# The first load of queries and keys in one transfer or in five, before an attention and two MoE layers on one core

## The chip, the core and the metric

One core of a Trainium2 chip runs one program. The metric is the device time of one execution in microseconds (us), as a median over runs. Beside the timed runs there is one execution taken with the hardware profiler; all rows below come from that one.

## The reference, cut to what matters

Inputs are float32. Attention has 2 batches of 12 heads, 448 positions and head size 64, with a causal mask. Its output, 896 tokens of 768 features, goes through two feed-forward layers that are plain matrix products.

```python
scores = (1 / sqrt(64)) * q @ k.T;  scores[above the diagonal] = -1e9
attn = exp(scores - max);  attn = attn / (sum(attn) + 1e-9)
x = attn @ v                                    # (896, 768) over all heads
h = x @ w_in;  g = max(h, 0) + alpha * min(h, 0);  x = g @ w_out      # 768 -> 2048 -> 768
h = max(x @ w1, x @ w2, x @ w3);  out = h @ w_out2                    # 768 -> 768 -> 768
```

## The kernel before, in words

The kernel takes the attention in 12 jobs, one for each pair of heads (class `Job`, line 560). A pair sits on the two halves of the 128 partitions: head 0 on rows 0 to 63 and head 1 on rows 64 to 127, 64 being the head size. The queries of a head are cut into four chunks, chunk 0 of 64 rows and chunks 1 to 3 of 128. Chunk `c` needs only the first 192, 320 or 448 keys (c = 1, 2, 3), since the mask hides the rest. For head 1 the keys are stored in reverse order.

A job loads one tile `qk` of 128 x 960 values (480 KB, line 681) and one tile `v` (line 685), both from the SyncE queue. Its scores (line 701) are products of 64 rows, both heads side by side, in groups of chunks. The first job takes its groups in the order 1, 2, 3, 0; the others take (3), (2, 1), 0. Chunk 0 of both heads is one pair of products over all 128 rows (`first_scores`, line 717). VectorE then takes the row maxima under the mask (line 735), ScalarE the exponentials (line 748), VectorE the reciprocals of the sums (lines 761 and 762), GpSimd scales the rows (line 766), TensorE transposes them (line 791), and the product with `v` follows (line 812). Scores go into four PSUM banks (`RINGS["s"]`), two for each group, so the third group waits until the maxima of the first have been read. The `qk` tile has three buffers.

After the attention come the feed-forward products (line 503), in two float32r parts for each operand. While the attention runs, the conversion of the first weights (lines 463 to 498) fills ScalarE, VectorE and GpSimd.

At the very start TensorE runs nine products of constants, 448 bfloat16 columns each (`warm`, line 877, `WARM = 9`). Nobody reads their result. Meanwhile GpSimd makes the identity and the masks (lines 277 to 305), and ScalarE loads its table for the exponential.

The order of instructions on every engine is fixed when the program is built, by a list planner (class `Plan`, line 76). Each step has a rank, a set of engines with its cost on each, the steps that it comes after, and the ring buffers that it takes and gives back. The planner keeps a clock for each engine and picks over and over the step that can start first, and of those that start within 0.02 us of each other the one of lowest rank. A step's `delay` is added after its cost before others may follow it. `NONE` is an engine without instructions. The chip does not know these times; it runs each engine's list in order and waits on semaphores. For a load of `qk` the planner reckons 0.05 + 480/285 = 1.73 us of SyncE and a delay of 1.8 us.

Two jobs are started ahead of the one whose probabilities are transposed (`LEAD = 2`). SyncE's list begins with `qk` of job 0, `qk` of job 1, `v` of job 0, `qk` of job 2 and `v` of job 1.

Of the kernel before, what the change touches and what calls it, by code (L numbers as in the profile page):

```python
# [11 lines left out]
F32 = mybir.dt.float32  # L12
# [11 lines left out]
RINGS = dict(w=4, s=4, t=3, a=1, v=4, qk=3, e=3, p=2)  # L24
LEAD = 2
NB = 3
HELD = 3
WARM = 9


RANK = dict(
    load=-6, v=12, s=12, max=12, exp=16, recip=10,
# [15 lines left out]
def f32(ap):  # L48
    return ap.bitcast(F32)


def step(fn, *args):
    return lambda engine: fn(*args)
# [6 lines left out]
def on_act(n, psum=False, words=False):  # L60
    return {"ACT": (0.056 if psum else 0.1) + n * (0.92e-3 if words else 0.833e-3)}
# [10 lines left out]
def on_dma(kb):  # L72
    return {"SP": 0.05 + kb / 285}
# [129 lines left out]
def attention_moe_moe2_kernel(  # L203
# [24 lines left out]
    nc = tc.nc  # L228
    B, HP = qk.shape[:2]
    D = 64  # L230
    DM, NT = out.shape
    S = NT // B
    DFF = alpha.shape[0] * alpha.shape[1]
    DF2 = w1.shape[0] * w1.shape[3]
    P = 128
# [8 lines left out]
    START = [0, *range(S % P, S + 1, P)]  # L244
# [19 lines left out]
    first = attn.enter_context(tc.tile_pool(name="first", bufs=1))  # L264
    ld = attn.enter_context(tc.tile_pool(name="ld", bufs=3))
# [16 lines left out]
    for j in range(2):  # L282
        nc.gpsimd.affine_select(
            out=short[P // 2 * j : P // 2 * j + P // 2],
            in_=short[P // 2 * j : P // 2 * j + P // 2],
# [7 lines left out]
    for j, o in enumerate((S - P, 0)):  # L293
# [3 lines left out]
            out=mask[:, o : o + P],  # L297
            in_=mask[:, o : o + P],
# [12 lines left out]
        delay=1.8,  # L311
# [222 lines left out]


    H = P // 2
    assert ROWS[0] == H and ROWS[1:] == [P] * (NCH - 1) and NCH == 4
    PLACES = [
        [1, 0, (0, 2, 3), (0, 0, 1), (0, 0, 2), (0, 0, 3), (0, 1, 2), (0, 1, 3)],
# [12 lines left out]

    e_all = [at.tile([P, 2 * NP - H], F32, bufs=1, name=f"e{i}") for i in range(RINGS["e"])]
    used = {"e": 0}

    def turn(name, tiles):
        used[name] += 1
        return tiles[(used[name] - 1) % len(tiles)]

    class Job:  # L560


        def __init__(self, rank, b, hp, after):
            self.b, self.hp, self.rank = b, hp, rank
            self.ps, self.pt, self.p = {}, {}, {}

            self.groups = ((1,), (2,), (3,), (0,)) if rank == 0 else ((3,), (2, 1), (0,))
            sums = ((1,), (2,), (3, 0)) if rank == 0 else ((3,), (2, 1, 0))
            self.sums = {cs[-1]: cs for cs in sums}
            self.slot = {c: k for k, c in enumerate(c for cs in sums for c in cs)}  # L570

            add = self.add
            self.load = add("load", on_dma(480), step(self.load_qk), take=("qk",), delay=1.8)
            self.norm, self.exps, self.max, s = {}, {}, {}, None
            for i, cs in enumerate(self.groups[:-1]):
                s = add(
                    "s",
                    {"PE": 4 * sum(START[c + 1] for c in cs) / 2400},
                    step(self.scores, i),
                    (self.load, *after) if s is None else (s,),  # L580
                    take=("s", "s") + ("e",) * (i == 0),
                    mode="rows",
                )
                if i == 0:
                    self.e_took = s
                if 3 in cs:
                    self.shared = s
                self.soften(s, cs, s)

            self.scored = s  # L590

        def add(self, kind, *args, **kw):
            return plan.add(self.rank + RANK[kind], *args, **kw)
# [40 lines left out]
        def turn(self, after, spare):  # L634
# [3 lines left out]
            for i in range(2):  # L638
# [11 lines left out]
                for k in range(2):  # L650
                    w = BANK if i == 0 or k else 6 * H
                    self.outs.append(
# [10 lines left out]
        def sum(self, after):  # L663
            add = self.add
            load_v = add("v", on_dma(448), step(self.load_v), take=("v",), delay=1.8)
            self.summed = a = add(
                "av",
                {"PE": 4 * (sum(S - START[kc + 1] for kc in range(NCH - 1)) + NCH * H) / 2400},
                step(self.av),
                [*self.outs, load_v, *after],  # L670
                take=("a",),
                give=(("p", self.p_took), ("v", load_v)),
                mode="columns",
            )
            hi, lo = (partial(self.x_out, i) for i in range(2))
            src = lambda: self.pv
            x = add("x", on_act(S, psum=True), copy(hi, src), (a,))
            self.done = add("x", on_dve(S, psum=True), sub(lo, src, hi), (x,), give=(("a", a),))

        def load_qk(self):  # L680
            self.qk = ld.tile([P, 2 * S + P // 2], F32, tag="qk", bufs=RINGS["qk"], name="qk")
            nc.sync.dma_start(out=self.qk, in_=qk[self.b, self.hp])

        def load_v(self):
            self.v = ld.tile([P, 2 * NCH - 1, 2, D], F32, tag="v", bufs=RINGS["v"], name="v")
            nc.sync.dma_start(out=self.v, in_=v[self.b, self.hp])

        def scores(self, i):
            if i == 0:
                self.e = e_all[used["e"] % len(e_all)]  # L690
                self.nm = at.tile([P, NCH, 2], F32, tag="nm", bufs=RINGS["e"], name="nm")
                self.sm = turn("e", sm_all)
                self.rm = at.tile([P, NCH, 2], F32, tag="rm", bufs=RINGS["e"], name="rm")
            banks = [ps_s.tile([P, BANK], F32, tag="s", name="ps") for _ in range(2)]
            o = 0
            for c in self.groups[i]:
                n = START[c + 1]
                for j in range(2):
                    d = slice(D * j, D * j + D)
                    self.ps[c, j] = banks[j][:, o : o + n]  # L700
                    nc.tensor.matmul(  # L701
                        self.ps[c, j],
                        self.qk[d, H + START[c] : H + START[c] + P],
                        self.keys(n, j)[d],
                        start=True,
                        stop=True,
                    )
                o += n
            if 3 in self.groups[i]:
                self.ps[0, 0] = banks[0][:, S:]  # L710

        def keys(self, n, j):
            return self.qk[:, 2 * S + H - n :] if j else self.qk[:, S + H : S + H + n]

        def first_scores(self):
            for j in range(2):
                nc.tensor.matmul(
                    self.ps[0, 0][H * j : H * j + H],
                    self.qk[:, H * j : H * j + H],
                    self.keys(H, j),  # L720
                    start=True,
                    stop=True,
                )
# [150 lines left out]
    def warm():  # L874
        ps = ps_a.tile([P, BANK], F32, tag="a", name="warm")[:, :S]
        for _ in range(WARM):
            nc.tensor.matmul(ps, ones[:, :P], ones, start=True, stop=True)  # L877

    plan.add(0, {"PE": WARM * 0.36}, step(warm), take=("a",), give=(("a", None),))
    places = [(b, hp) for b in range(B) for hp in range(HP)]  # L880
    jobs = []
    for i in range(-LEAD, len(places)):
        if i >= 0:
            jobs[i].turn([jobs[i - 1].summed] if i else [ready], "s" if i + LEAD < len(places) else "b")
        if i + LEAD < len(places):
            after = [jobs[i].turned] if i > 0 else [ready] if jobs else []
# [58 lines left out]
    rank = 1000  # L945
# [5 lines left out]
    for f in [*range(NB - HELD, NB), *(f for f in order if not NB - HELD <= f < NB)]:  # L951
        w = held[f] if NB - HELD <= f < NB else Weights(rank, w_in, 0, KC, f)
        us = [slice(EARLY.stop, NT)] if f < NB else [t for _, t in to_and_fro(f, CUT)]
        for u in us:
            after = w.ready + [j.done for j in jobs]
# [24 lines left out]
    for e in range(KC):  # L980
# [20 lines left out]
        for u, t in enumerate(CUT):  # L1001
# [3 lines left out]
            h = plan.add(rank, on_act(N, psum=True), copy(lambda dst=dst: dst(0), src), (prods[u].end,))  # L1005
# [41 lines left out]
    for f in range(KG):  # L1047
        ws = [Weights(rank, w, 0, KC, f) for w in (w1, w2, w3)]
        m, m_end, took = {}, [None] * B, None
        for i in range(3):  # L1050
            for u, cut in to_and_fro(KG + f + i + 1, CUT):
# [23 lines left out]
                if i == 0:  # L1075
# [5 lines left out]
                        take=("mx",) * (f >= KH and took is None),  # L1081
# [11 lines left out]
        k = f % KH  # L1093
        for u in range(B):
            if f < KH and u == 1:
# [3 lines left out]
            h = plan.add(  # L1099
                rank, on_act(S), copy(lambda dst=dst: dst(0), src), m_end if u else m_end[:1]  # L1100
            )
# [30 lines left out]
        c = slice(r * P, r * P + P)  # L1132
        if f % 2 == 0:
# [7 lines left out]
                after=(second,),  # L1141
# [4 lines left out]
        else:  # L1146
# [7 lines left out]
                after=(second,),  # L1154
# [5 lines left out]
            b = lambda n, w=w: f32(w.t)[:, n * KH : n * KH + KH]  # L1160
            d = lambda n, c=c: room["s"][n][:, :, c]
# [241 lines left out]
    for r in range(EH):  # L1403
# [7 lines left out]
            lambda engine, o, cols, a=a: copy(lambda: o, lambda: a.ps[:, cols])(engine),  # L1411
# [9 lines left out]
    for r in range(EH):  # L1421
# [5 lines left out]
        c, d, b, e = (Bank() for _ in range(4))  # L1427
        p5 = mul(rank, c, 0, r, 0)
        p6 = mul(rank, d, 1, r, 1, give=(("w", boxes[2 * r]["took"]),))
        x = {}  # L1430
# [5 lines left out]
        def u3(b=b, x=x):  # L1436
# [12 lines left out]
            lambda engine, o, cols, c=c, x=x: nc.vector.tensor_tensor(  # L1449
                out=o, in0=c.ps[:, cols], in1=x["b"][:, cols], op=ALU.add  # L1450
            ),
# [9 lines left out]
            lambda engine, o, cols, e=e, x=x: nc.vector.tensor_tensor(  # L1461
                out=o, in0=x["b"][:, cols], in1=e.ps[:, cols], op=ALU.subtract
            ),
# [12 lines left out]
            lambda engine, o, cols, c=c, x=x: nc.vector.tensor_tensor(  # L1476
                out=o, in0=c.ps[:, cols], in1=x["a"][:, cols], op=ALU.add
            ),
# [82 lines left out]
```

## Times and profile before

| | us |
|---|---|
| runs | 480.97, 482.00, 481.98 |
| median | 481.98 |
| profiled execution | 481.8 |
| its span, first to last instruction | 479.9 |

The profiled execution's own time is 1.9 us above its span; that part lies around the instructions. TensorE is busy for 472.2 us of the span. DMA moves 58.7 MB, 122 GB/s over the span. The page's 40 slices are 12 us each; the first one has TensorE at 8 tenths, the second to the last but one at 9, the last at 7.

### The profile page before, as it was taken

The numbers are of one execution on the slowest core, as the hardware profiler recorded it, in microseconds if no ns is written. First come the engines' busy times: TensorE is split into PE (matmuls) and PEld (weight loads), VectorE is DVE, ScalarE is ACT, GpSimd is POOL, SyncE is SP. The second block draws the span as 40 slices with busy tenths as digits, with TensorE's granted clock in tenths as the row PEclk, the third lists the DMA queues.
The fourth block names the chain that finished last, engine by engine and source line by source line (L and its number), as shares of the span: only waits on it lengthen the run. The fifth ranks groups of instructions, "written<-read, shape, count | busy, mean of one in ns | idle before, by whom it ended". The sixth has DMA issues, their size and how long they took to land.

```text
span 479.9 us, 7767 instructions
## 1 busy us (share of the span) xinstructions
PE 472.2 (98%) x2919; PEld 410.3 (85%) x2919; DVE 388.6 (81%) x766; ACT 250.1 (52%) x481; POOL 62.8 (13%) x109
## 2 busy tenths in 40 slices
PE   8999999999999999999999999999999999999997
PEld 4776677889998889999998888998899998899896
DVE  5999999999999999755756657589999998716952
ACT  6999996454535544443433434454565654306500
POOL 5655785011000000000000000020100000000000
PEclk9999999999999999999999999999999999999999
DMA  7775323324323323423334234345454533000122
GB/s 273 251 258 190 121 68 100 136 94 131 131 73 126 133 65 113 133 97 120 111 96 146 70 106 142 121 132 197 132 177 158 185 139 131 2 0 2 57 96 78
DMA packets 13861, 58.70 MB, mean 122 GB/s; under 512 B 1664, under 2 KB 3328, under 8 KB 13824
## 3 DMA queue, kind: packets, MB, share of 16 engines
q1 hardware_dynamic: 13680, 58.11, 36.4%
q8 instruction: 23, 0.38, 0.3%
q14 instruction: 14, 0.11, 0.1%
q10 hardware_dynamic: 144, 0.10, 0.1%
HBM read 55.45 MB, written 2.75 MB: 121 GB/s over the span
## 4 chain that ended last, share of the span: by engine, by line
PE 88%; DVE 7%; POOL 2%; issue 1%; ACT 1%; DVEq 0%; POOLq 0%
PE ps L503 79%; PE ps L701 3%; PE pv L812 3%; PE pt L791 2%; POOL e L766 2%; DVE xl L331 2%; DVE e L735 1%; PE warm L877 1%; ACT e L748 1%; DVE wl L331 1%; DVE t L1039 1%; DVE p L325 0%; DVE v L1222 0%; DVE v L1250 0%; ACT p L319 0%
## 5 line engine op out<-in xcount | busy, mean ns | idle before, releaser
L503 PE MATMUL ps<-xh,wl 128*128 128x384 f32 (+2 forms) x435 | 158.1, 363 | 0.0
L503 PE MATMUL ps<-xh,wh 128*128 128x384 f32 (+2 forms) x435 | 158.0, 363 | 0.0
L503 PE MATMUL ps<-xl,wh 128*128 128x384 f32 (+2 forms) x435 | 157.9, 363 | 0.0
L503 PEld LDWEIGHTS ps<-xh,wh 128*128 128x128 f32 x435 | 81.7, 188 | 9.1
L503 PEld LDWEIGHTS ps<-xl,wh 128*128 128x128 f32 x435 | 81.7, 188 | 8.8
L503 PEld LDWEIGHTS ps<-xh,wl 128*128 128x128 f32 x435 | 81.6, 188 | 8.5
L319 ACT CAST wh<-t 128x768 fp32r<-128x768 f32 (+2 forms) x53 | 41.8, 789 | 65.0 <-DVE t L498 58.5
L503 PE MATMUL ps<-g_h,wl 128*128 128x512 f32 (+1 forms) x192 | 69.7, 363 | 0.0
L503 PE MATMUL ps<-g_l,wh 128*128 128x512 f32 (+1 forms) x192 | 69.6, 363 | 0.0
L503 PE MATMUL ps<-g_h,wh 128*128 128x512 f32 (+1 forms) x192 | 69.5, 362 | 0.0
L331 DVE TENSOR_TENSOR wl<-t,wh 128x768 fp32r<-128x768 f32 (+2 forms) x54 | 49.5, 916 | 17.3 <-ACT wh L319 17.3
L463 ACT ACTIVATE t<-raw 128x768 f32<-128x768 f32 (+2 forms) x61 | 51.9, 853 | 15.5 <-DMA raw<-in_moe_w_dram 9.8
L487 DVE SCALAR_TENSOR_TENSOR t<-raw,t 128x768 uint32<-128x768 uint32 (+2 forms) x61 | 56.6, 930 | 0.8
L482 ACT ACTIVATE r<-raw 128x768 uint32<-128x768 uint32 (+2 forms) x61 | 51.8, 848 | 2.6 <-DMA raw<-in_moe_w_dram 1.7
L498 DVE CUSTOM_DVE_ANT_0 t<-t,r 128x1536 uint16<-128x1536 uint16 (+2 forms) x53 | 48.4, 913 | 2.3
L748 ACT ACTIVATE e<-e,nm 128x192 f32<-128x192 f32 (+3 forms) x84 | 44.1, 530 | 4.1 <-DVE nm L735 3.7
L766 POOL TENSOR_SCALAR e<-e,rm 128x192 f32<-128x192 f32 (+3 forms) x84 | 43.2, 536 | 22.4 <-DVE rm L762 9.4
L498 POOL TENSOR_TENSOR t<-t,r 128x384 int32<-128x384 int32 (+1 forms) x8 | 13.3, 1668 | 243.2 <-DVE t L487 241.3
L319 ACT CAST g_h<-g 128x384 fp32r<-128x384 f32 (+1 forms) x32 | 18.2, 569 | 45.4 <-DVE g L850 45.4
L503 PEld LDWEIGHTS ps<-g_l,wh 128*128 128x128 f32 x192 | 36.0, 188 | 3.9
L503 PEld LDWEIGHTS ps<-g_h,wh 128*128 128x128 f32 x192 | 36.1, 188 | 3.9
L503 PEld LDWEIGHTS ps<-g_h,wl 128*128 128x128 f32 x192 | 36.0, 188 | 3.8
(102 smaller groups left out, 547.6 us busy)
## 6 DMA issues: line engine op xcount, KB each, us to landing
raw<-in_moe_w_dram SPq DMA_DIRECT2D x18, 768.0 KB, 4.3
raw<-in_moe_w_in_dram SPq DMA_DIRECT2D x16, 768.0 KB, 4.3
raw<-in_moe_w_out_dram SPq DMA_DIRECT2D x12, 768.0 KB, 4.4
raw<-in_moe_w_out_dram SPq DMA_DIRECT2D x12, 640.0 KB, 4.1
qk<-in_qk_dram SPq DMA_DIRECT2D x12, 480.0 KB, 4.2
v<-in_v_dram SPq DMA_DIRECT2D x12, 448.0 KB, 4.3
out_dram<-o SPq DMA_DIRECT2D x11, 224.0 KB, 1.9
out_dram<-o SPq DMA_DIRECT2D x1, 128.0 KB, 1.7
```

The costliest lines, as they stand in the source:

```text
L319: nc.scalar.copy(out(), src())
L331: ENGINE[engine].tensor_tensor(out=out(), in0=a(), in1=f32(b()), op=ALU.subtract)
L463: nc.scalar.activation(out=f32(self.t[:, c]), in_=f32(self.raw[:, c, :, 1]), func=AF.Abs)
L482: nc.scalar.activation(out=self.r[:, c], in_=self.raw[:, c, :, 0], func=AF.Copy, scale=2.0**-29)
L487: nc.vector.scalar_tensor_tensor(out=self.t[:, c], in0=self.raw[:, c, :, 1], scalar=0xC0000000, in1=self.t[:, c], op0=ALU.bitwise_and, op1 ...
L498: ENGINE[engine].tensor_tensor(out=t, in0=t, in1=self.r[:, c].bitcast(I32), op=ALU.add)
L503: nc.tensor.matmul(ps, a, c, start=(first and y == 0), stop=(last and y == 2), **kw)
L701: nc.tensor.matmul(self.ps[c, j], self.qk[d, H + START[c] : H + START[c] + P], self.keys(n, j)[d], start=True, stop=True,)
L748: nc.scalar.activation(out=s, in_=s, func=AF.Exp, scale=-1.0, bias=self.column(self.nm, c, j), accum_out=self.column(self.sm[..., 0], c, j),)
L766: ENGINE[engine].tensor_scalar(out=s, in0=s, scalar1=self.column(self.rm, c, j), scalar2=1.0, op0=ALU.mult, op1=ALU.mult,)
L791: nc.tensor.transpose(banks[r][:, o : o + H], self.e[at_row, s : s + P], ident[at_row, at_row])
L812: nc.tensor.matmul(pv[D * j : D * j + D, q:end], self.v[:, k, j, :], self.p[:, at_col[j] : at_col[j] + end - q], start=(i == 0), stop=(i = ...
```

## The change

The first job's `qk` is no longer loaded by one transfer but by five, issued in one planner step: two from SyncE (rows 0 to 63, head 0) and three from ScalarE (rows 64 to 127, head 1). The columns of the tile are laid out anew for all jobs, so that the first transfer of each head (320 columns, 80 KB) holds what chunk 1 needs. The planner is told that this load has a delay of 0.7 us instead of 1.8, and that the later score groups of the first job start no earlier than a step `rest` on the engine without instructions, which takes 1.0 us after the load. `WARM` goes from 9 to 6. The host's arrangement of the inputs follows the new layout; it isn't timed.

```diff
-WARM = 9
+WARM = 6
...
+    END = 2 * S - H
...
-            self.load = add("load", on_dma(480), step(self.load_qk), take=("qk",), delay=1.8)
+            if rank:
+                self.load = add("load", on_dma(480), step(self.load_qk), take=("qk",), delay=1.8)
+                rest = ()
+            else:
+                self.load = add("load", on_dma(480), step(self.load_pieces), take=("qk",), delay=0.7)
+                rest = (add("load", {"NONE": 1.0}, lambda engine: None, (self.load,)),)
...
-                    (self.load, *after) if s is None else (s,),
+                    (self.load, *after) if s is None else (s, *rest),
...
+        def load_pieces(self):
+            self.qk = ld.tile([P, 2 * S + P // 2], F32, tag="qk", bufs=RINGS["qk"], name="qk")
+            n = P + START[2]
+            for j, cols in (
+                (0, slice(0, n)),
+                (1, slice(END - n, END)),
+                (0, slice(n, END + P)),
+                (1, slice(0, END - n)),
+                (1, slice(END, END + P)),
+            ):
+                queue = nc.scalar if j else nc.sync
+                rows = slice(D * j, D * j + D)
+                queue.dma_start(out=self.qk[rows, cols], in_=qk[self.b, self.hp, rows, cols])
...
-                        self.qk[d, H + START[c] : H + START[c] + P],
+                        self.queries(c, j)[d],
...
-            return self.qk[:, 2 * S + H - n :] if j else self.qk[:, S + H : S + H + n]
+            return self.qk[:, END - P - n : END - P] if j else self.qk[:, P : P + n]
+
+        def queries(self, c, j):
+            o = (END - P if j else 0) if c == 1 else P * (c - 2) + (0 if j else P + S)
+            return self.qk[:, o : o + P]
...
-                    self.qk[:, H * j : H * j + H],
+                    self.qk[:, END + H * j : END + H * j + H],
```

Here `n` is 320 and `END` is 832. The five transfers hold 80, 80, 160, 128 and 32 KB, in the order of the list.

## Rows read from the trace of the kernel before

**Rows 1.** The page: busy time by engine, then the chain's shares by engine.
```profile
PE 472.2 (98%) x2919; PEld 410.3 (85%) x2919; DVE 388.6 (81%) x766; ACT 250.1 (52%) x481; POOL 62.8 (13%) x109
...
PE 88%; DVE 7%; POOL 2%; issue 1%; ACT 1%; DVEq 0%; POOLq 0%
```

**Rows 2.** Busy time by stretch: stretch, length, each engine's busy us (instructions), clock, DMA.
```profile
0.00:11.20 11.20, 9.11 (x53) 4.63 (x53) 5.78 (x35) 6.72 (x20) 5.95 (x20) 1.00 0.79 268
11.20:37.70 26.50, 26.48 (x370) 19.25 (x370) 24.63 (x106) 26.00 (x87) 15.48 (x32) 1.00 0.74 255
37.70:79.10 41.40, 39.23 (x529) 29.16 (x525) 39.90 (x146) 39.40 (x118) 28.84 (x53) 1.00 0.36 120
79.10:450.00 370.90, 370.90 (x1842) 333.52 (x1841) 302.01 (x452) 174.99 (x253) 12.57 (x7) 1.00 0.34 113
```

**Rows 3.** The chain that ended last, its first 12 us: start, us, what.
```profile
0.77 3.52 PE warm L877 x9
4.29 0.71 PE ps L701 x4
...
6.88 0.52 DVE e L735
...
7.46 0.34 PE ps L717 x4
7.80 1.00 PE ps L701 x4
...
11.18 0.94 PE pt L791 x22
```

**Rows 4.** Timeline, weight loads: start, us, engine, line, operation [idle before, releaser].
```profile
4.22 0.76 PEld L701 LDWEIGHTS ps<-qk 64*128 64x128 f32 x8 [0.73 <-DMA qk<-in_qk_dram]
```

**Rows 5.** The tile `qk` up to 6 us: its three loads.
```profile
L682 SPq DMA_DIRECT2D qk<-in_qk_dram x3: 372/417/432, 0.7 to 2.1; - x3
...
DMA to landing us min/median/max: 3.2/4.0/6.7
```

**Rows 6.** Timeline of ScalarE and of the issues on SyncE, first 6 us.
```profile
0.73 1.28 ACT L748 ACT_TABLE_LOAD   x1 [0.73 <-PEq L1540]
0.74 0.84 SPq L682 DMA_DIRECT2D qk<-in_qk_dram  x2
1.63 0.42 SPq L686 DMA_DIRECT2D v<-in_v_dram  x1
...
5.50 0.46 ACT L748 ACTIVATE e<-e,nm 128x192 f32<-128x192 f32 x1 [3.48 <-DVE nm L735]
```

**Rows 7.** Busy time by half microsecond; the last two columns are DMA share and GB/s.
```profile
2.00:2.50 0.50, 0.50 (x3) 0.15 (x1) 0.00 (x0) 0.01 (x1) 0.45 (x1) 1.00 0.45 169
2.50:3.00 0.50, 0.50 (x3) 0.18 (x2) 0.00 (x0) 0.00 (x0) 0.43 (x3) 1.00 1.01 399
3.00:3.50 0.50, 0.50 (x3) 0.26 (x2) 0.00 (x0) 0.00 (x0) 0.43 (x2) 1.00 1.07 430
```

**Rows 8.** DMA issues in the last 10 us: KB each, median us to landing.
```profile
out_dram<-o ACTq DMA_DIRECT2D x1, 96.0 KB, 1.7
```

**Rows 9.** The opening products: ns min/median/max, first and last start.
```profile
L877 PE MATMUL warm<-const-bfloat16-1.0 x9: 531/577/577, 0.8 to 3.7; 128*128 128x448 bf16 x9
```

**Rows 10.** TensorE by shape from 0 to 6 us: busy us, mean ns.
```profile
L701 PE MATMUL ps<-qk 64*128 64x192 f32 x4 | 0.7, 442 | 0.0
L701 PE MATMUL ps<-qk 64*128 64x320 f32 x4 | 0.7, 429 | 0.0
```

**Rows 11.** TensorE by shape from 12 to 66 us.
```profile
L701 PE MATMUL ps<-qk 64*128 64x192 f32 x40 | 8.2, 324 | 0.0
```

**Rows 12.** Timeline of VectorE, the row maxima of the first job.
```profile
5.10 0.36 DVE L735 CUSTOM_DVE_ANT_0 e<-ps,mask 128x192 f32<-128x192 f32 x1 [4.08 <-PE ps L701]
...
5.66 0.49 DVE L735 CUSTOM_DVE_ANT_0 e<-ps,mask 128x320 f32<-128x320 f32 x1
...
6.79 0.60 DVE L735 CUSTOM_DVE_ANT_0 e<-ps,mask 128x448 f32<-128x448 f32 x1
```

**Rows 13.** Timeline of GpSimd, the last step of the masks.
```profile
3.37 0.29 POOL L296 TENSOR_SCALAR_AFFINE_SELECT mask<-mask 128x128 f32<-128x128 f32 x1
```

**Rows 14.** Busy time in two later stretches.
```profile
38.00:40.00 2.00, 1.59 (x34) 1.18 (x32) 1.63 (x7) 2.00 (x8) 2.00 (x6) 1.00 0.63 181
60.00:80.00 20.00, 18.64 (x249) 14.76 (x246) 19.50 (x60) 17.99 (x49) 14.46 (x23) 1.00 0.25 80
```

More of the change, by code (lines that the diff above doesn't have):

```diff
@@ L1522 @@
         first[:, :, j, :, j] = q[:, :, j, :, :64]
-    inputs["qk"] = _np.concatenate(
-        [first.reshape(b, h // 2, 2, d, 128), q[..., 64:], k], axis=-1
+    q1, q2 = q[..., 64:192], q[..., 192:]
+    inputs["qk"] = _np.stack(
+        [
+            _np.concatenate(x, axis=-1)
+            for x in (
+                (q1[:, :, 0], k[:, :, 0], q2[:, :, 0], first[:, :, 0].reshape(b, h // 2, d, 128)),
+                (q2[:, :, 1], k[:, :, 1], q1[:, :, 1], first[:, :, 1].reshape(b, h // 2, d, 128)),
+            )
+        ],
+        axis=2,
     ).reshape(b, h // 2, 2 * d, -1)
```

## The prediction, made before the changed kernel was run

> **What bounds the kernel now.** I read the page first. TensorE is busy for 98% of the span and carries 88% of the chain that ended last [rows 1], so a saving anywhere else counts only where TensorE stands still. The busy time by stretch says where that is [rows 2]: of 11.2 us at the start TensorE works 9.11, then 26.48 of 26.5, then 39.23 of 41.4, and from 79 to 450 us it never stops. The change touches the first stretch. In the chain of that stretch [rows 3] the reader is to see that TensorE is named until 4.29 us with work that no output needs, the opening products; then come the first scores, VectorE's maxima until 7.46, the scores of job 1, and at 11.18 the transposes, from where TensorE is solid. So all that ends earlier at about 7.5 us moves the whole program, unless the middle stretch takes it back.
>
> What holds the first scores at 4.22 us? The row of the weight load says the DMA of `qk` [rows 4]. That load is issued at 0.74 and lands 3.2 later (the least of the three, and nothing is queued ahead of it), at 3.94 [rows 5, 6]. The scores start 0.28 later. The opening products end then too: nine of them, started (3.7 - 0.8)/8 = 0.37 us apart [rows 9], are in the chain until 4.29. So two things end together here, and taking one away alone would bring little: the change has to move both, and does.
>
> **The change part by part.**
>
> *Three opening products fewer.* 3 x 0.37 = 1.1 us. TensorE is free for scores at 4.22 - 1.1 = 3.12 or before.
>
> *The first two pieces.* 160 KB in place of 480 must land before the scores of chunk 1. From above, they land no later than the whole does now, 3.94. From below, the nearest row is the one transfer on ScalarE's queue, 96 KB, a store, 1.7 us to landing [rows 8]: 2.44. My value comes from the load itself: once it runs, DMA moves 399 to 430 GB/s [rows 7], so 320 KB less, 328 thousand bytes at 415 GB/s, are 0.79 us less: 3.15. With the same 0.28 behind it the scores start at 3.43 (bounds 3.12 and 4.22).
>
> The DMA page of the Trainium skill speaks against this ("DMA: Bandwidth & Descriptors", section "Rules for kernel authors"): two transfers to the two halves of the partitions use the same 16 engines, so one ought to take a single transfer over 128 partitions. By that rule the second queue adds no rate, and rows 7 agree: one queue already moves 430 GB/s. The rule leaves open whether a smaller first piece lands sooner; if not, the result is rival E.
>
> *The first scores at the lower clock.* The clock column reads full from the start, but the opening products contradict it: 448 columns in 0.37 us are 1.2 GHz [rows 9]. The first four products of 192 columns took 442 ns in the mean [rows 10], later ones 324 [rows 11], and the 320-column ones after them 429: the clock rose while the first scores ran, so near 4.5 us, after 3.7 us of unbroken work. Now the scores run before that point. From weight load to VectorE's first maximum were 5.10 - 4.22 = 0.88 us [rows 4, 12]; all at the lower level I add 0.1: 0.98, so 4.41. VectorE needs 5.66 - 5.10 = 0.56 for the two maxima of chunk 1 [rows 12] and is free at 4.97. That is 0.69 earlier than before.
>
> *Pieces three and four.* Chunk 2 needs them, so its scores get a wait that they did not have. Behind it stand, on TensorE, chunk 3, chunk 0 and all of job 1; VectorE waits for them. By then 448 of the 480 KB have moved: 3.94 - 32 KB/415 GB/s = 3.86, plus 0.28 = 4.14. Its four products took 0.7 us [rows 10] and VectorE follows some 0.1 later (4.29 + 0.71 against 5.10 [rows 3, 12]): 0.8 at full clock. The first 0.4 us lie below full clock and cost about 0.2 more: 1.0, so VectorE starts chunk 2 at 5.14 and not at 5.66. Gain 0.52. The bounds: 0.69 where VectorE is late and not the data; with the lower clock all through, 0.7 becomes 1.25, the start 5.49 and the gain 0.17. I take 0.5, as the pieces are the same bytes as before and should end at the same time.
>
> *From there.* The maxima of chunk 3, chunk 0 and job 1 follow in VectorE's order at unchanged cost, so the 0.5 is handed to 7.46. What would be late next is not close: `qk` of job 1 is issued one SyncE issue later (0.42 [rows 6]), but its bytes stood behind the first load's anyway; it landed at 1.16 + 4.0 = 5.2 [rows 5] and is needed at 7.8 - 0.5. The third `qk` landed at 2.1 + 6.7 = 8.8, before the transposes at 11.18, and `v` after it is later still.
>
> *Costs taken at nothing.* ScalarE issues three transfers, 3 x 0.42 = 1.3 us by SyncE's rows. If its table load (1.28) follows, it is done at 0.73 + 1.3 + 1.28 = 3.3; the first exponential, at 5.50 now, is due at 4.8 [rows 6]. Cover 1.5 us. The masks are done at 3.66 [rows 13], the first maximum is due at 4.41: cover 0.75, and with the lower bound of the start still 0.4. The new layout changes addresses, not shapes. Waits on five semaphores in place of one lie within the 0.28.
>
> *The planner.* It now believes that the first scores start 1.1 us earlier (delay 0.7 for 1.8) and chunk 2's about 0.5 earlier (2.43 + 1.0 against 3.53 + 0.42), while SyncE's list, and with it the arrival of the first weights, stays where it was. Weight conversions therefore slide against the attention's steps, and the order may change wherever starts were close. I take nothing for it in the sum and keep both signs for the range.
>
> **Sum.** 481.8 - 0.5 = **481.3**, by the profiled execution's own time. The median of the runs shown, 481.98, lies 0.2 above that execution.
>
> **The rivals.**
>
> *A. More is gained.* Pieces land nearer to the lower bound, the scores start at 3.12 and VectorE paces all: its first maximum at 4.10, chunk 2 at 4.66, 1.0 earlier than 5.66. For it: the row of the 96 KB transfer. Against it: pieces three and four would have to land at 3.4 to 3.6, with two thirds of a load's bytes still to come at 3.15. Time 480.8, or lower with a lucky order.
>
> *B. The order in the middle stretch.* From 37.7 to 79.1 us TensorE stands for 2.17 us [rows 2] with VectorE and ScalarE over 95% busy, and 1.36 of that lies between 60 and 80 [rows 14]. If a conversion slips ahead of a step of the attention there, one such block of stalls comes on top: 481.3 + 1.4 = 482.7, and slower than before from 0.5 on. It can also go away: 480.0. For it: full engines and shifted plans. Against it: where all is late by the same amount, the order stays.
>
> *C. The clock rises later.* Fewer opening products, then a gap of some 0.3 us before the scores and another before chunk 2. If TensorE stays at 1.2 GHz until about 9 us, chunk 2 gains only 0.17, and the 0.34 and 1.00 us that the chain has of TensorE from 7.46 on [rows 3] grow to at most double. About 1.1 lost: 482.7. Against it: the gaps are short beside the work around them. It decides once it costs over 0.5.
>
> *D. The change doesn't do what it says:* ScalarE's transfers go out behind its table load, at 2.02 and not at 0.73 [rows 6]. Head 1's first piece then lands at 2.02 + 2.4 = 4.4, its second at about 4.9, and chunk 2 starts 0.3 later than before: 482.1. The trace has nothing on ScalarE between table load and exponential, so it cannot tell the order. The skill's page "ScalarE: Activation LUTs" (section "Step-by-step: what each stage is for") puts the table load right before the activation that needs it, hence behind the transfers; no run here shows it yet.
>
> *E. Pieces land no sooner than the whole:* the engines interleave them and all end near 3.94. Then the scores start at 4.22 as before: 481.8. The page on DMA says of several queues that they interleave; rows 7 show a rate and not an order.
>
> **How the numbers follow.** Forecast 0.34 (own range 480.9 to 481.7), A 0.26, B slower 0.13 and faster 0.07, C 0.07, D 0.05, E 0.08. The range 480.0 to 482.7 takes in all but the tails of B and C and a little more for the runs' own spread of 1.0 us. About 0.2%, 0.96 us, is what a measurement of this kernel tells from no change. Faster by more: B's good side, half of A and a fifth of the forecast with its order in luck, 0.07 + 0.15 + 0.08, and some spread: 0.34. Slower by more: B's bad side and half of C: 0.17. The rest, 0.49, is within.
>
> **What would show it.** First weight load of scores near 3.4 with ScalarE's issues from 0.73 on and the table load behind them; VectorE's first maximum near 4.4, chunk 2's near 5.1 with a gap before it; first products of chunk 0 at 6.95; transposes solid from 10.7; idle time of TensorE between 37.7 and 79.1 still near 2.2. Wrong, if the first weight load stays at 4.2 (E), ScalarE's issues stand behind 2.0 (D), products of job 1 take twice their time (C), or that idle time moves by more than 0.5 (B).

## The result

The changed kernel is slower: 484.51 us in the median of ten runs (481.8 to 485.39), the kernel before 481.88 (480.97 to 482.36). The ratio is 1.0051, 95% interval 1.0039 to 1.0063, so 2.6 us. The new kernel's runs also spread over 3.6 us where the old one's spread over 1.4; the experiments come back to that. The profiled execution took 484.16 us, its span 482.3.

The chain of waits of the changed kernel, its first 14 us (start, us, what), against [rows 3]:

```profile
0.73 0.57 SPq L702
1.30 0.06 issue
1.36 3.69 DMA qk<-in_qk_dram
5.05 0.04 issue
5.09 2.94 PE ps L721 x7
...
8.74 0.48 PE ps L741 x4
9.22 1.85 PE ps L721 x4
...
13.45 0.94 PE pt L815 x22
```

A DMA now stands in the chain where the opening products stood: SyncE's second piece, issued at 1.36, takes 3.69 us to land at 5.05. The transposes, from which TensorE is solid, start at 13.45 and no longer at 11.18: 2.27 us later, with a span 2.4 longer. So nearly all of the loss is made before 13.5 us. The busy time by stretch agrees: TensorE stands 2.15 of the 41.4 us from 37.7 on, as before (2.17 [rows 2]).

```profile
11.20:37.70 26.50, 26.32 (x357) 18.98 (x355) 24.42 (x105) 25.30 (x81) 16.30 (x33) 1.00 0.74 248
37.70:79.10 41.40, 39.25 (x532) 29.16 (x529) 39.97 (x150) 39.32 (x125) 28.99 (x52) 1.00 0.39 135
```

The timeline of weight loads, ScalarE and VectorE, against [rows 4, 6, 12]:

```profile
3.15 0.80 PEld L721 LDWEIGHTS ps<-qk 64*128 64x128 f32 x4 [0.78 <-DMA qk<-in_qk_dram]
...
5.09 1.96 PEld L721 LDWEIGHTS ps<-qk 64*128 64x128 f32 x8 [1.13 <-DMA qk<-in_qk_dram]
```

```profile
0.73 2.13 ACTq L702 DMA_DIRECT2D qk<-in_qk_dram  x3
...
2.89 1.28 ACT L772 ACT_TABLE_LOAD   x1 [2.89 <-issue]
...
4.31 0.36 DVE L759 CUSTOM_DVE_ANT_0 e<-ps,mask 128x192 f32<-128x192 f32 x1 [3.29 <-PE ps L721]
...
6.56 0.49 DVE L759 CUSTOM_DVE_ANT_0 e<-ps,mask 128x320 f32<-128x320 f32 x1 [1.59 <-PE ps L721]
...
8.05 0.62 DVE L759 CUSTOM_DVE_ANT_0 e<-ps,mask 128x448 f32<-128x448 f32 x1 [0.33 <-PE ps L721]
```

Up to 4.31 all went better than forecast: the scores of chunk 1 start 1.07 us earlier than before, their first maximum 0.79 earlier. Then VectorE waits 1.59 us. The maxima of chunk 2 are 0.90 later than before, those of chunk 3 1.26.

The pieces, issued up to 2.5 us (KB, median us to landing), against [rows 5, 8]:

```profile
qk<-in_qk_dram SPq DMA_DIRECT2D x1, 160.0 KB, 3.7
qk<-in_qk_dram ACTq DMA_DIRECT2D x1, 128.0 KB, 4.1
qk<-in_qk_dram ACTq DMA_DIRECT2D x1, 80.0 KB, 2.7
qk<-in_qk_dram SPq DMA_DIRECT2D x1, 80.0 KB, 2.4
qk<-in_qk_dram ACTq DMA_DIRECT2D x1, 32.0 KB, 4.8
```

Busy time by half microsecond (last two columns DMA share and GB/s), against [rows 7]:

```profile
2.50:3.00 0.50, 0.50 (x2) 0.00 (x0) 0.00 (x0) 0.11 (x1) 0.43 (x3) 1.00 0.85 205
3.00:3.50 0.50, 0.50 (x3) 0.35 (x3) 0.00 (x0) 0.50 (x1) 0.43 (x2) 1.00 1.13 244
```

The engines are as busy as before and move half: 205 and 244 GB/s where one transfer moved 399 and 430. In this microsecond they worked off 148 packets of 0.22 MB in all, where it had been 121 packets of 0.41 MB. With 16 engines, busy for 0.99 and 1.04 of it, that is 0.107 us of an engine for a packet in place of 0.138, though a packet held less than half as much.

TensorE by shape, the products of job 1, from 9.1 to 12.6 us in the changed kernel (busy us, mean ns), and from 7.6 to 9.6 in the kernel before:

```profile
L721 PE MATMUL ps<-qk 64*128 64x448 f32 x4 | 1.9, 1032 | 0.0
L721 PE MATMUL ps<-qk 64*128 64x320 f32 x4 | 1.3, 737 | 0.0
L721 PE MATMUL ps<-qk 64*128 64x192 f32 x4 | 0.7, 446 | 0.0
```

```profile
L701 PE MATMUL ps<-qk 64*128 64x448 f32 x4 | 1.0, 588 | 0.0
L701 PE MATMUL ps<-qk 64*128 64x320 f32 x4 | 0.7, 429 | 0.0
L701 PE MATMUL ps<-qk 64*128 64x192 f32 x4 | 0.5, 322 | 0.0
```

The same instructions last up to 1.75 times as long. That is TensorE's lower level, 1.2 GHz by the opening products [rows 9], until the last products of this group, at about 12.3 us; in the kernel before it was left at about 4.5. The clock column reads 1.00 in both kernels and shows none of it, because it counts time for which the trace has no record of the clock as full. The record itself begins with the rise, at 4.53 us in the kernel before and at 12.28 in the changed one, and the durations change at the same points.

### The profile page after: what moved, and what is told of

The parts are those of the page before. It is cut to its first block, busy times and chain, and to the rows that moved or that the text cites. A ratio compares the mean times of both kernels' runs of the same rounds, so it can differ in the third digit from the quotient of the medians.

```text
span 482.3 us, 7765 instructions
## 1 busy us (share of the span) xinstructions
PE 474.5 (98%) x2916; PEld 411.9 (85%) x2916; DVE 388.7 (81%) x766; ACT 250.2 (52%) x481; POOL 62.8 (13%) x109
## 4 chain that ended last, share of the span: by engine, by line
PE 88%; DVE 6%; POOL 2%; issue 1%; ACT 1%; DMA 1%; SPq 0%; DVEq 0%; POOLq 0%
PE ps L503 79%; PE ps L721 4%; PE pv L836 3%; POOL e L790 2%; PE pt L815 2%; DVE xl L331 2%; DVE e L759 1%; DMA qk<-in_qk_dram 1%; ACT e L772 1%; DVE wl L331 1%; DVE t L1063 1%; DVE p L325 0%; DVE v L1246 0%; DVE v L1274 0%; ACT p L319 0%
```

## The experiments

Two things are late, then, pieces and clock; the planner's new order is the third suspect. All kernels below keep the changed kernel's order of steps; they differ in the products of constants and in how the first load is cut and laid out. "Before" is always the kernel before, timed beside them. The kernels e5 to e8 ran on another chip than the other experiments.

**Nine opening products again** (e1_nine).

```diff
-        for _ in range(WARM):
+        for _ in range(9):
```

> The changed kernel with nine opening products again, everything else and the whole order as in the changed kernel. Clock theory: TensorE works without a break until about 4.1 us and on into the first scores, the clock rises near 4.5 us as in the kernel before, and the products of job 1 last what they lasted before (448 columns: about 560 ns and not 990). Only the late pieces remain (chunk 2 at about 5.1 instead of 4.8): 482.0 to 482.4 beside 481.9 before. Theory of the late pieces: nothing changes against the changed kernel, about 484.5. Theory of the order: the same, about 484.5.

Measured: 482.10 beside 481.58, ratio 1.0014 (1.0004 to 1.0024); one run of twelve lies above 483. That is what the clock theory had expected. The pieces are late here too, and later than in the changed kernel: the one of 160 KB lands 4.3 us after its issue and not 3.7, and TensorE stands 0.79 us for chunk 2. But job 1 runs at the higher level, twelve products in 1.89 us where the changed kernel takes 3.42:

```profile
4.22 0.65 PE L721 MATMUL ps<-qk 64*128 64x192 f32 x4
5.66 2.40 PE L721 MATMUL ps<-qk 64*128 64x320 f32 x8 [0.79 <-DMA qk<-in_qk_dram]
8.45 0.34 PE L741 MATMUL ps<-qk 128*64 128x64 f32 x4 [0.39 <-DVE nm L759]
8.71 1.89 PE L721 MATMUL ps<-qk 64*128 64x448 f32 x12
```

Three products that no output needs give back 2.1 of the 2.6 us. The late pieces and the order together account for 0.5.

**One transfer, six opening products** (e2_one_load).

```diff
-                self.load = add("load", on_dma(480), step(self.load_pieces), take=("qk",), delay=0.7)
+                self.load = add("load", on_dma(480), step(self.load_qk), take=("qk",), delay=0.7)
```

> The changed kernel with the first load in one transfer from SyncE again; six opening products and the planner's order stay. Clock theory: TensorE stands from about 3.1 to 4.2 us, the clock rises late, near 8 to 12 us, and the time is 483.5 to 485. Theory of the late pieces: all is as before the change, 481.9, as the load lands at 3.9 again. Theory of the order: 484.5.

Measured: 483.36, all five runs from 483.08 to 483.81, ratio 1.0041 (1.0028 to 1.0054), just under the clock theory's 483.5 to 485.

**One transfer, nine opening products**, both edits together (e3_plan_only):

> Of the change only the planner's new order and the new layout stay: the first load in one transfer and nine opening products. Clock theory and theory of the late pieces: as before the change, 481.9 within 0.3. Theory of the order: 484.5.

Measured: 481.77, ratio 1.0007 (0.9998 to 1.0015), no run above 482.15. So the planner's order costs 0.2 us in the median, and nothing that the interval tells from zero. The pair is the cleanest one: the same load in the same order, and only three constant products more or less, while TensorE waits for DMA anyway. First the timeline with six, then with nine:

```profile
0.77 2.40 PE L901 MATMUL warm<-const-bfloat16-1.0 128*128 128x448 bf16 x6 [0.77 <-PEq L1572]
4.07 3.71 PE L721 MATMUL ps<-qk 64*128 64x192 f32 x12 [0.90 <-DMA qk<-in_qk_dram]
8.37 0.48 PE L741 MATMUL ps<-qk 128*64 128x64 f32 x4 [0.58 <-DVE nm L759]
8.78 3.57 PE L721 MATMUL ps<-qk 64*128 64x448 f32 x12
```

```profile
0.77 3.52 PE L901 MATMUL warm<-const-bfloat16-1.0 128*128 128x448 bf16 x9 [0.77 <-PEq L1572]
4.22 3.13 PE L721 MATMUL ps<-qk 64*128 64x192 f32 x12
8.15 0.34 PE L741 MATMUL ps<-qk 128*64 128x64 f32 x4 [0.80 <-DVE nm L759]
8.42 1.89 PE L721 MATMUL ps<-qk 64*128 64x448 f32 x12
```

With six, the scores start even 0.15 earlier, after a break of 0.90 us, and job 1 takes 3.57 us for 1.89. The clock is full from 13.71 us on with six and from 6.64 with nine. The later rise alone is worth 1.6 us (483.36 - 481.77).

**Four constant products behind the scores of chunk 1** (e4_fill).

```diff
+            if self.rank == 0 and i == 0:
+                ps = ps_a.tile([P, BANK], F32, tag="a", name="fill")[:, :S]
+                for _ in range(4):
+                    nc.tensor.matmul(ps, ones[:, :P], ones, start=True, stop=True)
```

> The changed kernel with four more products of constants right behind the scores of chunk 1, so that TensorE works through the wait for the pieces of chunk 2 (4.5 to 5.1 us); order otherwise as in the changed kernel. Clock theory: the clock rises near 4.5 us, chunk 2 starts at 5.1 at full clock, 0.3 later than before the change: 482.0 to 482.4. Theory of the late pieces: no better than the changed kernel, 484.5 or a little more. Theory of the order: 484.5.

A miss for the clock theory as I had put it: 484.32, ratio 1.0053 (1.0034 to 1.0072), with runs from 482.09 to 485.33; five of six were at 483 or more. The profiled execution, 483.06, is one of these five, and yet it had job 1 at the higher level:

```profile
5.97 2.07 PE L721 MATMUL ps<-qk 64*128 64x320 f32 x8
...
9.30 1.89 PE L721 MATMUL ps<-qk 64*128 64x448 f32 x12
```

Its clock was full from 6.94 us on, and TensorE shows no break before chunk 2. What made it late is mostly the data: the 160 KB piece landed 4.5 us after its issue (3.7 in the changed kernel), and the scores of chunk 2 began at 5.97 and not at 5.09. So a time above 483 does not by itself show the lower clock. The other four runs, 483.84 to 485.33, have no profile; whether the clock stayed low in them is not shown.

**All five pieces on SyncE** (e5_sync_only).

```diff
-                queue = nc.scalar if j else nc.sync
+                queue = nc.sync
```

> The changed kernel with all five pieces on SyncE's queue; order and six opening products stay. Theory that two queues get in each other's way: one after the other on one queue, the pieces end where the whole ended, the fourth by about 4.1 us instead of 5.4, chunk 2 starts near 4.3, TensorE has no long break after 3.2 us, and the time is 481.5 to 483. Theory that small transfers are slow in themselves: the fourth lands at 5 or later, and the time stays near 484.

Measured: 483.15 (481.63 to 483.98), ratio 1.0032 (1.0019 to 1.0045). One queue doesn't bring the pieces in: the 128 KB piece, issued at 2.62, lands 2.8 us later at 5.4. It is late for another reason than with two queues, where it was issued at 1.34 and took 4.1. The five issues of 64 rows last 0.57 to 0.60 us each where the 480 KB had 0.37, so the pieces leave 0.63 us apart; each then lands 2.3 to 3.0 us after its issue, not much less than the 3.2 of the whole load. From 2.5 to 4.0 us the DMA engines are busy for only 0.35 to 0.70 of the time. The profiled execution, 481.63, gives a second pair for the clock, full here from 4.11 us on:

```profile
3.10 1.38 PE L721 MATMUL ps<-qk 64*128 64x192 f32 x4
5.05 1.99 PE L721 MATMUL ps<-qk 64*128 64x320 f32 x8 [0.57 <-DMA qk<-in_qk_dram]
...
7.92 1.89 PE L721 MATMUL ps<-qk 64*128 64x448 f32 x12
...
11.37 0.94 PE L815 MATMUL pt<-ident,e 64*128 64x64 f32 x22 [0.15 <-POOL e L790]
```

Scores at 3.10 and 5.05, as in the changed kernel (3.15 and 5.09), on TensorE the same instructions; but transposes at 11.37 and not 13.45, and a span of 479.8 and not 482.3. With the clock up early, the late pieces cost this one execution hardly more than the early first piece had gained (481.63 beside 481.32).

**Two halves, whole rows, two queues, nine opening products** (e6_halves).

```diff
...
+            for j, cols in ((0, slice(0, END + P)), (1, slice(0, END + P))):
...
```

> The first load in two transfers of 64 rows and all 960 columns, one from SyncE and one from ScalarE, with nine opening products. It measures the two queues without small pieces. Theory of the two queues: SyncE goes on to the load of job 1 while ScalarE's half is still moving, so that half lands at 4.6 us or later where the whole landed at 3.9, and the time is 0.3 to 1.0 above the kernel before. Theory of the small transfers: both halves land by about 4.0, and the time is that of before.

Measured: 482.78 (482.22 to 484.22), ratio 1.0032 (1.0019 to 1.0045). Issued side by side at 0.73, the halves land a microsecond apart:

```profile
qk<-in_qk_dram SPq DMA_DIRECT2D x1, 240.0 KB, 3.6
qk<-in_qk_dram ACTq DMA_DIRECT2D x1, 240.0 KB, 4.6
```

The second lands at 5.3 where the whole landed at 3.94. So two halves on two queues cost too, with rows of full length; which of the two it is, the queue or the halves, this run does not separate. This is what the Trainium skill warns of ("DMA: Bandwidth & Descriptors", section "Rules for kernel authors": use one transfer over 128 partitions instead of two over its halves), and the trace agrees with it, 1.4 us in this place.

The time is 1.5 us above the kernel before, more than either theory allowed. The profiled execution, at 484.22 the longest of the five, has a late rise of the clock in it:

```profile
4.37 4.56 PE L714 MATMUL ps<-qk 64*128 64x192 f32 x12
...
9.44 3.57 PE L714 MATMUL ps<-qk 64*128 64x448 f32 x12
```

Job 1 ran at the lower level and the clock was full only from 13.49 us on, although nine opening products had run and TensorE's rows show no break. From 4.37 to 5.36 us, though, only the two products of head 0 ran, and the weight loads waited 0.49 us for the second half; whether that held the clock down is not shown. So nine opening products do not secure an early rise.

**Three transfers over all 128 rows, one queue** (e7_wide with six opening products, e8_wide_seven with seven). The columns are laid out so that what chunk 1 needs is the same 320 columns for both heads.

```diff
...
+            for cols in (slice(2 * P, 2 * P + 320), slice(2 * P + 320, END + P), slice(0, 2 * P)):
+                nc.sync.dma_start(out=self.qk[:, cols], in_=qk[self.b, self.hp, :, cols])
...
```

> The first load in three transfers over all 128 rows on SyncE's queue alone, the first with the 320 columns that chunk 1 of both heads needs (another layout of the columns); six opening products. Both theories on the transfers: pieces land in turn, the first by about 3.2 us, the last by 4.2; chunk 1 starts near 3.3 and chunk 2 near 4.3, and TensorE has only short breaks. Clock theory: since TensorE works nearly without a break, the clock rises as in the kernel before, and the gain that the prediction worked out, 0.5 us, comes: 481.2 to 481.6 where the kernel before has 481.9; where the breaks are enough to keep the clock low, 483 to 484.

> As the kernel with three transfers over 128 rows, with seven opening products: they end near 3.5 us, behind the landing of the first transfer, so that no break is left between them and the scores. Clock theory: the clock rises as before the change in all runs, the scores start 0.7 us earlier than before, and the time is 481.0 to 481.6 where the kernel before has 481.9. If the break between opening products and scores does not matter, it is no better than with six.

Measured: 484.03 with six (ratio 1.0050, 1.0037 to 1.0063), 481.71 with seven (1.0017, 1.0003 to 1.0030). The third transfer, rows of 1024 bytes, lands near 5.0 all the same (issued at 1.64, 3.3 us), against both transfer theories' 4.2. With one more opening product the median is 2.3 us lower, and runs of 483 or more fall from three of five to three of twelve: a hint, from few runs, and the expectation of 481.0 to 481.6 in all runs failed. Both profiled executions, 481.98 and 481.96, had an early rise, the one with six even with a break of 1.01 us before chunk 2 (0.72 with seven), and neither shows TensorE idle ahead of the scores. What the executions at 484 looked like, they cannot show.

**Seven opening products and two between chunk 1 and chunk 2** (e10_wide_fill).

> The kernel with three transfers over 128 rows and seven opening products, and two more products of constants between the scores of chunk 1 and chunk 2, where TensorE stood for 0.72 us. Clock theory: the break is gone, the runs at 483 to 484 (four of twelve without the two products) are gone too, and the median is 481.4 to 481.9, chunk 2 starting at 5.1 to 5.3. If breaks have no part in it, runs at 483 to 484 stay as frequent as they were.

Measured: 482.01, ratio 1.0017 (1.0004 to 1.0029). One run of eleven is left above 483, which so few runs cannot tell from three of twelve. The median is not better than without the fillers: chunk 2 starts at 5.35, behind them.

**Two transfers over all 128 rows, long rows** (e9_two_wide), seven opening products.

```diff
...
+            for cols in (slice(0, 2 * P + 320), slice(2 * P + 320, END + P)):
+                nc.sync.dma_start(out=self.qk[:, cols], in_=qk[self.b, self.hp, :, cols])
...
```

> The first load in two transfers over all 128 rows on SyncE's queue, 288 KB with all that chunk 1 needs and 192 KB with the rest, and seven opening products. Theory of the small transfers: with long rows (2304 and 1536 bytes) the second lands by about 4.3 us, chunk 2 starts near 4.5 where it started at 4.8 before the change, and TensorE has no break of over 0.3 us. With the clock theory the time is then 481.0 to 481.6 in all runs where the kernel before has 481.4. If the number of transfers counts and not their size, the second lands near 4.1 as well; if any cut costs a microsecond, it lands near 5, chunk 2 starts at 5.1, and some runs lie at 483 to 484.

Measured: 481.34, all eleven runs from 481.16 to 481.71, beside 481.55 (480.74 to 482.21); ratio 1.0001 (0.9991 to 1.0010). Rows of 2304 and 1536 bytes land at 3.4 and 4.0:

```profile
qk<-in_qk_dram SPq DMA_DIRECT2D x1, 288.0 KB, 2.7
qk<-in_qk_dram SPq DMA_DIRECT2D x1, 192.0 KB, 2.8
```

```profile
3.52 2.99 PE L712 MATMUL ps<-qk 64*128 64x192 f32 x12
7.45 0.34 PE L732 MATMUL ps<-qk 128*64 128x64 f32 x4 [0.94 <-DVE nm L750]
7.71 1.89 PE L712 MATMUL ps<-qk 64*128 64x448 f32 x12
```

Fewer transfers and longer rows both fit the landing at 4.0; this run does not separate them. No break before chunk 2, no run above 481.71, and yet no gain over the kernel before: the scores start 0.70 earlier, at the lower clock, which lasts until 5.66 us (4.53 in the kernel before), and by chunk 0 (7.45 against 7.46 [rows 3]) the gain is spent. This is the best cut that I found. It repairs the change and doesn't beat the kernel before.

**The changed kernel once more** (e11_after_again).

> The changed kernel once more, for a second profile. Clock theory: where the time is 483.5 or more, the products of job 1 last about 990 ns (448 columns) and the transposes start at 13 us or later; where it is under 482.5, they last about 560 and the transposes start near 11.5, with the pieces landing at the same times in both.

Measured: 483.7.

```profile
3.18 5.09 PE L721 MATMUL ps<-qk 64*128 64x192 f32 x12
...
8.61 3.57 PE L721 MATMUL ps<-qk 64*128 64x448 f32 x12
```

Job 1 is at the lower level again and the clock full from 12.44 us on, as the clock theory had it; its numbers were a little off (448-column products of 916 ns in the mean, first transposes at 12.51). Two things differ from the first profile. The 160 KB piece lands 3.1 us after its issue and not 3.7, so the pieces do not land at the same times. And TensorE's rows show no break before chunk 0, only weight loads that waited 0.43 and 0.31 us for pieces: a break of 0.63 us is not needed for a late rise.

All kernels by runs of 483 us or more, beside what the profiled execution shows: its time, the break of TensorE between opening products and chunk 2, and the moment from which the trace has the clock at full.

| kernel | runs at 483 or more | profiled, us | break, us | clock full from, us |
|---|---|---|---|---|
| before, nine | 0 of 77 | 481.8 | none | 4.53 |
| one transfer, nine | 0 of 11 | 481.77 | none | 6.64 |
| two wide, seven | 0 of 11 | 481.34 | none | 5.66 |
| five pieces, nine | 1 of 12 | 482.32 | 0.79 | 4.37 |
| three wide, seven, two fillers | 1 of 11 | 481.78 | none | 5.30 |
| three wide, seven | 3 of 12 | 481.96 | 0.72 | 4.78 |
| two halves, nine | 2 of 5 | 484.22 | none | 13.49 |
| SyncE only, six | 5 of 10 | 481.63 | 0.57 | 4.11 |
| three wide, six | 3 of 5 | 481.98 | 1.01 | 3.93 |
| four fillers, six | 5 of 6 | 483.06 | none | 6.94 |
| changed kernel, six | 9 of 10 | 484.16 | 0.63 | 12.28 |
| changed kernel again, six | 1 of 1 | 483.7 | none | 12.44 |
| one transfer, six | 5 of 5 | 483.36 | 0.90 | 13.71 |

The moments fall into two groups, 3.9 to 6.9 and 12.3 to 13.7 us, and every profiled time above 483.1 goes with the second. The break does not sort them: the longest, 1.01 us, had an early rise, and two executions without a break a late one. The number of opening products shifts the odds: with six, 28 of 37 runs are at 483 or more, with seven 4 of 34, with nine 3 of 105. These counts mix different transfers; the two pairs that change nothing but six into nine are 9 of 10 against 1 of 12 (five pieces) and 5 of 5 against 0 of 11 (one transfer).

## Why the prediction was wrong

*Opening products and first pieces:* right. TensorE was free at 3.12 by the sum; the scores started at 3.15 (forecast 3.43, bound 3.12), with the first pieces down at 0.73 + 2.4 = 3.1 and, by the same rows, 3.4. Rival E is out.

*The first scores at the lower clock:* the maximum came at 4.31 (forecast 4.41), but by two errors that nearly cancel: from weight load to maximum it took 1.16 us and not 0.98, and the start was 0.28 early.

*Pieces three and four:* the first step that failed. "The same bytes as before and should end at the same time", 3.86, was the mistake: they landed at 5.05 and 5.4. The sum took the rate of one transfer with rows of 3840 bytes for pieces with rows of 512 to 2560. Rows 7 showed 430 GB/s for that one shape and nothing for others; what bounded the step in the text, the clock alone, left out the transfer. Chunk 2 began at 5.09 and not at 4.14, 0.95 us late at this point of the chain.

*"The first 0.4 us lie below full clock":* the second, and the larger. It took the moment at which the clock rose in one execution, 4.53 us, for a fixed time, while the change removed a third of the opening products; in the changed kernel's two profiles the clock rose at 12.28 and 12.44. From weight load to maximum chunk 2 took 6.56 - 5.09 = 1.47 us and not 1.0 (the bound was 1.35), and "at unchanged cost" failed for job 1, whose products took 3.42 us and not 1.89. This is rival C, to which I gave 0.07; its price of 1.1 was too low as well. By the pair of one transfer with six and with nine products, it is 1.6 us of the 2.6; the late pieces with nine products, order included, are 0.5. The rest, 0.5, appears only with both together, and was not taken apart.

*Costs taken at nothing:* the table load stood behind ScalarE's transfers, and ended at 4.17, before the first exponential. It was later than the 3.3 of the text, as three issues took 2.13 us and not 1.3: the cover of 1.5 us shrank to some 0.5. Rival D is out. The place of the load is the one that the Trainium skill gives ("ScalarE: Activation LUTs", section "Step-by-step: what each stage is for": right before the activation that needs it), and the trace agrees: it starts at 2.89, behind the transfers.

*The planner:* rival B is out. The order alone measured 1.0007 (0.9998 to 1.0015), and in the changed kernel the middle stretch kept its idle time, 2.15 us for 2.17.

*Rival A* had the start of the scores right (3.12, and 3.15 came), but pieces three and four would have had to land at 3.4 to 3.6. In the chances for "faster by more", half of A is 0.13 and a fifth of the forecast 0.07, not 0.15 and 0.08; no other number rests on it.

What is shown is that three opening products more, and nothing else, bring the times of an early rise back in most runs, and what that is worth; the rise itself is seen in one profile of each kernel, two of the changed one. What stays open is what decides it in a single execution: neither the break before chunk 2 nor the number of opening products does so alone. No kernel was profiled in both of its outcomes; the nearest to that is the pair of the changed kernel and its version on one queue. Not separated either is how much of the changed kernel's spread is the clock and how much the landing of its pieces, which moved by 1.4 us between executions.

## What to carry to other kernels

Work that no output needs, run while TensorE waits for its first data, can be worth more than the wait that it seems to fill: before taking it away, ask at which clock the next products will run, and read that from their durations. A sum that starts data earlier must take the rate and the issue times of transfers of the same row length and number; cutting one load into five halved the rate, and what chunk 2 needed came more than a microsecond later than the whole load had. If a first load is to be cut, few pieces over all partitions with long rows on one queue were the only cut that cost nothing here; they gained nothing either. And a kernel whose times fall into two groups needs a profile from each: a profile from one says nothing of the other.

## What the hardware showed that I had not expected

- The moment of the clock's rise is not fixed by the number of opening products or by TensorE standing still. With nine of them and no break in TensorE's rows it came at 4.53, 6.64 and 13.49 us (before, one transfer, two halves). The kernel with all pieces on SyncE ran once with it early (481.63) and five times in ten at 483.5 to 484.0, without a change in its instructions; the latter have no profile.
- The same five transfers on the same two queues landed at different times. The 160 KB piece took 3.7, 4.3, 4.5 and 3.1 us from issue to landing in four profiled executions (changed kernel, nine opening products, four fillers, changed kernel again), the 128 KB piece 4.1, 5.1, 4.7 and 4.0.
- The issue of a transfer of 64 rows lasted 0.57 us on both queues, up to 0.88 on ScalarE's, where one of 128 rows had 0.37 to 0.43 [rows 5]. The number of rows is not all of it: in the changed kernel the two loads of 128 rows of `qk` issued behind the pieces took 0.58 and 0.53.
- Seven tenths of a microsecond lost before the transposes need not reach the end: with one transfer and nine products the transposes started at 11.86 in the profiled execution, 0.68 later than before, and the span was 480.0, 0.1 longer; from 37.7 to 79.1 us TensorE stood for 1.71 us there and not 2.17.
